# Loads of shifted rows of k from a padded, slice-major copy in DRAM

## The chip, the cores and the metric

The kernel runs on one core of one Trainium2 chip. The metric is the device time of one execution in microseconds (us), as the median of several runs. TensorE is called PE, VectorE DVE, ScalarE ACT, GpSimd POOL and SyncE SP, as in the profile.

## The reference

The reference is one training step of a block: its output and the gradients of nine inputs. With S = 2048 rows, D = 1024 columns and F = 3584:

```python
xn = layernorm(q)                                   # q is also the residual input x
k_shift = sum over t of k_pad[:, t:t+S, :] * shift_k[:, 3 - t]    # k padded by 3 zero rows ahead
kv = k_shift * v
y  = irfft(rfft(kv, 2S) * rfft(ssm_k, 2S))[:S] + kv * ssm_D       # a causal convolution, per column
s  = xn * y
g  = silu(((xn @ w_gate) * (xn @ w_up)) @ w_down)
out = q + s * g
```

`reference` returns `out` and, from `grad_out`, the gradients by q, k, v, shift_k, ssm_k, ssm_D, w_gate, w_up and w_down. All inputs are bf16. k, v and q are [1, 2048, 1024].

What matters here is `k_shift`: row s of it needs the rows s-3, s-2, s-1 and s of k, and the gradient by shift_k needs the same four rows again.

## The kernel before, in words

Rows are laid over the 128 partitions as "(c u r)": half c (2), partition u (128), row r within it (8). So partition u holds 8 consecutive rows of a half, and a tile with shifted rows holds 11: the 8 and the 3 ahead of them.

The program has five stages. The matmuls of each stage are on PE; the convolution's work is threaded through them by a "pump", a generator that is advanced a little at each tick of the main loop.

- Layer norm and the first gate/up units (`layer_norm`, `gu_unit`, lines 399 to 471, called from lines 569 to 587). For each quarter q of the rows, SP loads x, DVE and ACT normalize it, PE transposes it into `XNT`, POOL stores it to `XNd`, and four gate/up units run on that quarter. The x tiles have two buffers, so that a later load waits until an earlier tile has been stored. `build_bcast` (line 124) makes the broadcast weights `Wbc` and `Dbc`; `build_tables` (line 143) makes the transform tables.
- Gate/up matmuls (line 455), with `conv_forward` (line 473) in the pump. The columns are taken in 4 pairs of slices (dp), 8 slices (ds) of 128 columns. `shift(dp)` (line 492) makes acc = k_shift and kv for 256 columns, in two halves c; `load_kv` (line 479) loads k and v for the next half when one is done; `main(ds)` transforms a slice and multiplies, `tail(ds)` ends it. The tile `k` is [128, 11, 256], with one buffer.
- Down projection (line 785), with the pointwise backward and the first part of `conv_backward` in the pump.
- The weight gradients: dh and the gradients of gate and up (lines 891 and 909), then the gradient of w_down (line 952): 56 groups of 16 matmuls into a PSUM bank `psdw`, which ACT copies to a tile `wb` (two buffers) and POOL stores. In the pump runs the rest of `conv_backward` (line 640), and at its end, beside the groups of line 952, `dk_load` (line 727) and `dk_unit` (line 738) for the 8 slices. `dk_load` loads the 11 shifted rows of k (`kh`) and of the gradient of k_shift (`dkh`, from the padded DRAM buffer `DKSHd`) for both halves; each has two buffers. `dk_unit` makes the gradient of k on DVE, in a tile `dka` that has one buffer and is stored half by half, and the gradient of shift_k by 16 matmuls on PE (`psY`, line 755).
- The gradient by q (line 1005).

The loads of k go through `cld_k` (line 64). `cld` is the same as `st` (line 59): a DMA issued by POOL, as all stores are. `ld` (line 56) issues on SP. For half c = 1, `cld_k` issues two DMAs over 128 partitions, for tile rows 0 to 5 and 6 to 10. For c = 0 the first three rows would lie ahead of k, so partition 0 is done apart: a memset of its rows 0 to 2 on DVE, a DMA of one partition for its other 8 rows, and two DMAs over the 127 partitions from 1. Each run in DRAM is one row's w columns: 512 bytes for w = 256, 256 bytes for w = 128.

The framework orders the instructions of each engine itself by a list scheduler with a cost estimate of its own; an engine's queue then runs in that order. So an instruction that stands late in the source (a load of k, a copy) can come early on its engine.

Of the kernel before, what the change touches and what calls it, by code (L numbers as in the profile page):

```python
# [13 lines left out]
BF16 = mybir.dt.bfloat16  # L14
# [5 lines left out]
def build_kernel(  # L20
# [8 lines left out]
    nc = tc.nc  # L29
# [61 lines left out]
    KSHd = dram.tile([4, P, NB, 256], BF16, name="KSHd")  # L91
    KVd = dram.tile([4, P, NB, 256], BF16, name="KVd")
# [31 lines left out]
    def build_bcast(bps):  # L124
# [15 lines left out]
        st(DKSHd[:, S:S + 8, :], zr[:])  # L140
        bsb.release()
# [331 lines left out]
    def conv_forward():  # L473
# [5 lines left out]
        def load_kv(dp, c):  # L479
            d0 = dp * 256  # L480
# [3 lines left out]
            cld_v(v, c, d0, 256)  # L484
            S_["kv", dp, c] = (k, v)
# [6 lines left out]
        def shift(dp):  # L492
            d0 = dp * 256
            kv = cx.tile([P, NB, 256], BF16, name="kv", bufs=1)
            S_["kvt", dp] = kv
            wb = lambda j: Wbc[:, j:j + 1, d0:d0 + 256].to_broadcast([P, 8, 256])
            for c in range(2):
                k, v = S_.pop(("kv", dp, c))
                acc = kst.tile([P, 8, 256], BF16, name="acc")
                tt(acc[:], k[:, 0:8, :], wb(3), MUL)  # L500
                for j in (2, 1, 0):
                    prod = kst.tile([P, 8, 256], BF16, name="prod")
# [3 lines left out]
                tt(kv[:, 8 * c:8 * c + 8, :], acc[:], v[:], MUL)  # L506
                st(KSHd[dp, :, 8 * c:8 * c + 8, :], acc[:])
# [4 lines left out]
            st(KVd[dp], kv[:])  # L512
# [14 lines left out]
        def main(ds):  # L527
            if ds % 2 == 0:
                yield from shift(ds // 2)
            kvs = S_["kvt", ds // 2][:, :, (ds % 2) * P:(ds % 2 + 1) * P]  # L530
# [52 lines left out]
    for q in range(1, 4):  # L583
# [4 lines left out]
        if q == 1:  # L588
            pass
    lns.release()  # L590
    lnp.release()
    build_tables(ps_tr)
# [92 lines left out]
    def dkv_tail(ds, G, ew):  # L685
        e = ds % 2
        for c in range(2):
# [5 lines left out]
            cld(ksh[:], KSHd[ds // 2, :, 8 * c:8 * c + 8, e * P:(e + 1) * P])  # L693
# [422 lines left out]
```

## Time and profile before

| | |
|---|---|
| median of 3 runs | 2884.33 us (2872.3 to 2888.55) |
| the profiled execution | 2892.62 us, its span 2890.8 us |
| PE, DVE, ACT, POOL busy | 2250.8, 1446.9, 859.1, 782.8 us |
| mean granted clock of PE | 0.91 |
| DMA moved | 466.35 MB, 161 GB/s on the mean |
| first and last gate/up matmul (line 455) start | 87.2 and 886.2 us |
| first and last matmul of line 952 start | 1967.7 and 2426.9 us |

The profile is of one execution. A busy share is the time in which an engine had an instruction running. Groups of instructions are named by line, engine, operation and tile, "out<-in"; "<-" behind an idle time names what ended it. In the DMA issues the last number is the median time from issue to landing. The line numbers are those of the kernel before.

### The profile page before, as it was taken

How to read it: one execution, taken by the hardware profiler on the slowest of the kernel's cores; microseconds unless marked ns; L12 is line 12 of the kernel's file. 1: busy time of each engine (PE TensorE's matmuls, PEld its weight loads, DVE VectorE, ACT ScalarE, POOL GpSimd, SP SyncE). 2: the span in 40 equal slices, each digit the busy share in tenths (PEclk: the TensorE clock that was granted, in tenths of full speed). 3: DMA queues.
4: the chain of work that ended last, by engine and by line, in shares of the span. 5: the costliest groups of instructions: out<-in, count | busy, mean ns of one | idle time of the engine just before them, and what ended most of it. 6: DMA issues, size and time to landing. Idle time of an engine off the chain costs nothing.

```text
span 2890.8 us, 35638 instructions
## 1 busy us (share of the span) xinstructions
PE 2250.8 (78%) x14369; PEld 1200.7 (42%) x14634; DVE 1446.9 (50%) x1947; ACT 859.1 (30%) x1204; POOL 782.8 (27%) x990
## 2 busy tenths in 40 slices
PE   0573939859997988599999999999733454899998
PEld 0332515536563444355444554444311122444443
DVE  2532837758775568426775757657222222132222
ACT  1561314324442222343433433543200001221111
POOL 2242222232211433023344343222334432000000
PEclk9886979979998999799999999999866776999999
DMA  3422535354557998645566665555444445652320
GB/s 91 156 91 80 177 114 188 113 168 158 199 182 252 330 327 283 160 143 186 186 198 199 216 198 174 191 208 201 112 71 83 69 70 141 191 181 95 143 97 29
DMA packets 219237, 466.35 MB, mean 161 GB/s; under 512 B 42936, under 2 KB 128000, under 8 KB 206528
## 3 DMA queue, kind: packets, MB, share of 16 engines
q0 software_dynamic: 93440, 266.91, 29.7%
q1 hardware_dynamic: 121472, 195.06, 21.0%
q10 hardware_dynamic: 4160, 2.10, 0.3%
q8 instruction: 114, 1.87, 0.3%
q14 instruction: 51, 0.42, 0.0%
HBM read 273.15 MB, written 189.82 MB: 160 GB/s over the span
## 4 chain that ended last, share of the span: by engine, by line
issue 37%; PE 26%; DMA 13%; DVE 12%; POOL 8%; ACT 3%; POOLq 0%; SPq 0%; DVEq 0%; ACTq 0%
PE psdw L909 9%; DMA kh<-in_A_k_dram 4%; PE psbm L785 4%; DVE W L182 3%; PE psdw L952 3%; PE psdh L891 2%; PE psg L455 2%; POOL kh L60 2%; DMA HFd<-HX 2%; DVE m L182 1%; PE tr L902 1%; POOL out_dram L60 1%; DMA wrow<-DBMd 1%; DVE dgt L182 1%; DMA k<-in_A_k_dram 1%
## 5 line engine op out<-in xcount | busy, mean ns | idle before, releaser
L455 PE MATMUL psg<-XNT,wslab 128*128 128x512 bf16 x1708 | 414.7, 391 | 9.3 <-ACT XNT L442 4.4
L909 PE MATMUL psdw<-dgu,XN 128*128 128x512 bf16 x1740 | 396.7, 379 | 2.7
L952 PE MATMUL psdw<-DBMT,dgu 128*128 128x512 bf16 x874 | 206.0, 393 | 155.7 <-ACT wb L955 154.3
L1005 PEld LDWEIGHTS <-dgut 128*128 128x128 bf16 x1792 | 175.0, 98 | 224.1 <-DMA dgut<-DGUTd 16.7
L455 PEld LDWEIGHTS <-wslab 128*128 128x128 bf16 x1792 | 175.9, 101 | 203.3 <-issue 28.8
L909 PEld LDWEIGHTS <-XN 128*128 128x128 bf16 x1792 | 172.2, 98 | 192.3 <-issue 0.5
L60 POOL DMA_DIRECT2D out_dram<-wb x280 | 151.5, 546 | 295.3 <-ACT wb L913 188.8
L457 ACT CAST gut<-psg 128x512 bf16<-128x512 f32 x224 | 131.1, 586 | 304.6 <-PE psg L455 209.5
L891 PE MATMUL psdh<-DBMT,wdt 128*128 128x512 bf16 x858 | 213.2, 389 | 5.0 <-ACT dht L893 1.4
L182 DVE TENSOR_TENSOR W<-W 128x512 f32<-128x512 f32 (+1 forms) x272 | 213.3, 784 | 7.0
L785 PE MATMUL psbm<-wd,ht 128*128 128x512 bf16 x872 | 200.4, 384 | 9.8 <-DMA ht<-HTd 6.8
L952 PEld LDWEIGHTS <-dgu 128*128 128x128 bf16 x896 | 90.1, 101 | 266.3 <-issue 171.2
L182 DVE TENSOR_TENSOR W<-W,psP 128x512 f32<-128x512 f32 x192 | 122.3, 682 | 121.4 <-PE psP L231 72.5
L1005 PE MATMUL psx<-WGU,dgut 128*128 128x512 bf16 x748 | 168.3, 379 | 1.0
L955 ACT CAST wb<-psdw 128x512 bf16<-128x512 f32 x56 | 32.0, 585 | 395.0 <-DMA out_dram<-wb 284.2
L60 POOL DMA_DIRECT2D kh<-in_A_k_dram x40 | 113.0, 2828 | 128.8 <-issue 122.0
L903 ACT COPY dgu<-tr 128x1024 bf16<-128x1024 bf16 x112 | 113.4, 1012 | 103.0 <-PE tr L902 102.4
L913 ACT CAST wb<-psdw 128x512 bf16<-128x512 f32 x112 | 65.5, 586 | 248.4 <-PE psdw L909 213.3
L182 DVE TENSOR_TENSOR dkp<-dkh,Wbc 128x1024 bf16<-128x1024 bf16 x48 | 33.1, 689 | 208.7 <-DMA dkh<-DKSHd 207.6
L468 PE MATMUL tr<-ident,hT 128*128 128x128 bf16 x448 | 36.9, 224 | 124.4 <-DVE hT L182 123.0
L785 PEld LDWEIGHTS <-ht 128*128 128x128 bf16 x896 | 87.3, 99 | 109.4 <-DMA ht<-HTd 7.0
L1005 PE MATMUL psx<-XN,dgut 128*128 128x512 bf16 x501 | 116.8, 387 | 16.8 <-DMA dgut<-DGUTd 16.3
(217 smaller groups left out, 3339.2 us busy)
## 6 DMA issues: line engine op xcount, KB each, us to landing
ht<-HTd SPq DMA_DIRECT2D x16, 1792.0 KB, 7.8
gul<-GUTd SPq DMA_DIRECT2D x56, 512.0 KB, 4.9
DGUTd<-dgt POOLq DMA_DIRECT2D x56, 512.0 KB, 6.0
dgut<-DGUTd SPq DMA_DIRECT2D x8, 3584.0 KB, 11.9
GUTd<-gut POOLq DMA_DIRECT2D x48, 512.0 KB, 3.3
A<-DYFd POOLq DMA_DIRECT2D x16, 1024.0 KB, 5.5
out_dram<-wb POOLq DMA_DIRECT2D x224, 64.0 KB, 2.2
dgu<-Hd SPq DMA_DIRECT2D x28, 512.0 KB, 5.4
```

What stands on the lines that cost most here:

```text
L60: return nc.gpsimd.dma_start(out=out, in_=in_)
L182: V.tensor_tensor(o, a, b, op)
L455: nc.tensor.matmul(ps[:], w[:, dc, a, fi * P:(fi + 1) * P], XNT[q][:, dc, :], start=(dc == 0), stop=(dc == DC - 1))
L457: nc.scalar.copy(out=gut[:, a, k * 512:(k + 1) * 512], in_=ps[:])
L468: nc.tensor.transpose(ps[:, i, :], hT[:, i * P:(i + 1) * P], ident[:])
L785: nc.tensor.matmul(ps[:], ht[:, fc, i * P:(i + 1) * P], wds[fc // 4][:, fc % 4, :], start=(fc == 0), stop=(fc == NF - 1))
L891: nc.tensor.matmul(ps[:], wdt[:, dc, fi * P:(fi + 1) * P], DBMT[:, dc, s0:s0 + 512], start=(dc == 0), stop=(dc == DC - 1))
L903: nc.scalar.copy(out=dgu[:, :, a, fi * P:(fi + 1) * P], in_=ps[:])
L909: nc.tensor.matmul(ps[:].rearrange("p a f -> p (a f)"), XN[:, b, dc * P:(dc + 1) * P], dgus[b // 8][:, b % 8].rearrange("p a f -> p (a f)" ...
L913: nc.scalar.copy(out=wb[:], in_=ps[:])
L952: nc.tensor.matmul(ps[:], h[:, fi, b, :], DBM[:, b, dh * 512:(dh + 1) * 512], start=(b == 0), stop=(b == NB - 1))
L1005: nc.tensor.matmul(ps[:, dh * 512:(dh + 1) * 512], t[:, a, 4 * j + f, i * P:(i + 1) * P], WGU[j][:, a, f, dh * 512:(dh + 1) * 512], start= ...
```

## The change

A new DRAM buffer `KSLd` of [8, S + 8, 128] holds k by slices of 128 columns, with three zero rows ahead. Eight DMAs from DRAM to DRAM on SP fill it, one for each slice, in runs of 256 bytes at the source; they stand in the source behind the last layer norm and ahead of `build_tables`. One store of zeros by POOL in `build_bcast` fills the rows ahead. `cld_k` is now one DMA over 128 partitions, for either half, with 11 rows of 128 columns in one run of 2816 bytes for each partition; the memset and the one-partition load are gone.

What follows from the layout: the tile `k` is [128, 2, 11, 128] and is loaded by two DMAs, one for each slice of the pair; `shift` works on [128, 2, 8, 128]; `kv` is stored by slices; `KSHd` and `KVd` are by 8 slices of 128 columns and no longer by 4 pairs of 256, and `dkv_tail` and the pointwise stage read them so (`kv_t` by one DMA where there were two).

```diff
-    def cld_k(t, c, d0, w):
-        if c == 0:
-            nc.vector.memset(t[0:1, 0:3, :], 0.0)
-            cld(t[0:1, 3:11, :], kin[0:8, d0:d0 + w].rearrange("(o r) d -> o r d", o=1))
-        p0 = 1 - c
-        for (a, b) in ((0, 6), (6, 11)):
-            off = kin.offset + (1021 * c + 5 * (1 - c) + a) * D + d0
-            cld(t[p0:P, a:b, :], bass.AP(kin.tensor, off, [[8 * D, P - p0], [D, b - a], [1, w]]))
+    def cld_k(t, c, ds):
+        src = KSLd[ds]
+        cld(t, bass.AP(src.tensor, src.offset + 1024 * c * P, [[8 * P, P], [P, 11], [1, P]]))
...
-    KSHd = dram.tile([4, P, NB, 256], BF16, name="KSHd")
-    KVd = dram.tile([4, P, NB, 256], BF16, name="KVd")
+    KSHd = dram.tile([8, P, NB, P], BF16, name="KSHd")
+    KVd = dram.tile([8, P, NB, P], BF16, name="KVd")
+    KSLd = dram.tile([8, S + 8, P], BF16, name="KSLd")
...
         st(DKSHd[:, S:S + 8, :], zr[:])
+        st(KSLd[:, 0:3, :], zr[:, 0:3, :])
...
-            k = kst.tile([P, 11, 256], BF16, name="k")
-            cld_k(k, c, d0, 256)
+            k = kst.tile([P, 2, 11, P], BF16, name="k")
+            for e in range(2):
+                cld_k(k[:, e], c, 2 * dp + e)
...
-                    tt(prod[:], k[:, 3 - j:11 - j, :], wb(j), MUL)
+                    tt(prod[:], k[:, :, 3 - j:11 - j, :], wb(j), MUL)
...
-                st(KSHd[dp, :, 8 * c:8 * c + 8, :], acc[:])
+                st(KSHd[2 * dp:2 * dp + 2, :, 8 * c:8 * c + 8, :].rearrange("e u b d -> u e b d"), acc[:])
...
     lns.release()
     lnp.release()
+    for ds in range(8):
+        ld(KSLd[ds, 3:3 + S, :].rearrange("(p a) d -> p a d", a=16),
+           kin[:, ds * P:(ds + 1) * P].rearrange("(p a) d -> p a d", a=16))
     build_tables(ps_tr)
...
-            cld(ksh[:], KSHd[ds // 2, :, 8 * c:8 * c + 8, e * P:(e + 1) * P])
+            cld(ksh[:], KSHd[ds, :, 8 * c:8 * c + 8, :])
...
-            cld_k(kh[:, c], c, ds * P, P)
+            cld_k(kh[:, c], c, ds)
...
-            kv_t = mi.tile([P, 2, 2, 256], BF16, name="kv_t")
-            for e in range(2):
-                ld(kv_t[:, e], KVd[2 * dh + e, :, 2 * bp:2 * bp + 2, :])
+            kv_t = mi.tile([P, 4, 2, P], BF16, name="kv_t")
+            ld(kv_t[:], KVd[4 * dh:4 * dh + 4, :, 2 * bp:2 * bp + 2, :].rearrange("e u b d -> u e b d"))
```

How the change moves instructions is seen in the engines' order. On SP at the start of the program, before (x are the tiles of the layer norm, in_A_q the input q, wslab the weights of gate and up):

```order
L57 DMA x_135<-in_A_q_dram 128x1024
L57 DMA x_140<-in_A_q_dram 128x1024
L57 DMA x_228<-in_A_q_dram 128x2048
L57 DMA x_467<-in_A_q_dram 128x4096
L57 DMA x_686<-in_A_q_dram 128x4096
L57 DMA x_905<-in_A_q_dram 128x4096
```

and with the change (in_A_k is the input k, KSLd the copy):

```order
L57 DMA x_136<-in_A_q_dram 128x1024
L57 DMA x_141<-in_A_q_dram 128x1024
L57 DMA KSLd<-in_A_k_dram 2048x128 x5
L57 DMA x_229<-in_A_q_dram 128x2048
L57 DMA x_469<-in_A_q_dram 128x4096
L57 DMA KSLd<-in_A_k_dram 2048x128 x3
L57 DMA x_688<-in_A_q_dram 128x4096
L57 DMA x_907<-in_A_q_dram 128x4096
```

The eight copies, which stand behind all layer norms in the source, come on SP ahead of the third and of the fifth x load.

On POOL at the start, before (k is the tile of `load_kv`, XNd the stored layer norm):

```order
L60 DMA XNd<-x_135 128x1024
L60 DMA XNd<-x_140 128x1024
L60 DMA k<-in_A_k_dram 1x8x256
L60 DMA k<-in_A_k_dram 127x6x256
L60 DMA k<-in_A_k_dram 127x5x256
L60 DMA v<-in_A_v_dram 128x4x256 x2
L60 DMA hrow<-in_A_ssm_k_dram 128x2048
L60 DMA XNd<-x_228 128x2048
```

and with the change:

```order
L60 DMA XNd<-x_136 128x1024
L60 DMA XNd<-x_141 128x1024
L60 DMA KSLd<-zr 8x384
L60 DMA v<-in_A_v_dram 128x4x256 x2
L60 DMA hrow<-in_A_ssm_k_dram 128x2048
L60 DMA k<-KSLd 128x1408 x2
L60 DMA XNd<-x_229 128x2048
```

The first k loads are two DMAs over 128 partitions, which wait for the copies of slices 0 and 1 and for the zero rows, and stand behind v and hrow where they stood ahead.

On POOL at one of the slices of `dk_load`, before (wb is the tile of the w_down gradient, dka that of k's):

```order
L60 DMA kh<-in_A_k_dram 1x8x128
L60 DMA kh<-in_A_k_dram 127x6x128
L60 DMA kh<-in_A_k_dram 127x5x128
L60 DMA kh<-in_A_k_dram 128x6x128
L60 DMA kh<-in_A_k_dram 128x5x128
L60 DMA dkh<-DKSHd 128x1408 x2
L60 DMA out_dram<-wb 128x512 x2
L60 DMA out_dram<-dka 1024x1x128 x2
L60 DMA out_dram<-wb 128x512 x2
```

and with the change:

```order
L60 DMA kh<-KSLd 128x1408 x2
L60 DMA dkh<-DKSHd 128x1408 x2
L60 DMA out_dram<-wb 128x512 x2
L60 DMA out_dram<-dka 1024x1x128
L60 DMA out_dram<-wb 128x512 x2
L60 DMA out_dram<-dka 1024x1x128
```

Five loads of k become two for each slice; the stores of `wb` and `dka` alternate behind them as before, with the two halves of `dka` now apart. On PE the order there is the same but for the second slice, whose 16 matmuls of `psY` are no longer split: 64 matmuls of line 952 stand between one slice's `psY` and the next.

More of the change, by code (lines that the diff above doesn't have):

```diff
@@ L479, in load_kv @@
         def load_kv(dp, c):
-            d0 = dp * 256
-            k = kst.tile([P, 11, 256], BF16, name="k")
-            cld_k(k, c, d0, 256)
+            k = kst.tile([P, 2, 11, P], BF16, name="k")
+            for e in range(2):
+                cld_k(k[:, e], c, 2 * dp + e)
             v = kst.tile([P, 8, 256], BF16, name="v")
-            cld_v(v, c, d0, 256)
+            cld_v(v, c, dp * 256, 256)
             S_["kv", dp, c] = (k, v)
@@ L511, in shift @@
                 yield 2.5
-            st(KVd[dp], kv[:])
+            st(KVd[2 * dp:2 * dp + 2].rearrange("e u b d -> u e b d"), kv[:])
         def h_rows(ds):
@@ L529, in main @@
                 yield from shift(ds // 2)
-            kvs = S_["kvt", ds // 2][:, :, (ds % 2) * P:(ds % 2 + 1) * P]
+            kvs = S_["kvt", ds // 2][:, ds % 2]
             yield from h_rows(ds)
@@ L685, in dkv_tail @@
     def dkv_tail(ds, G, ew):
-        e = ds % 2
         for c in range(2):
@@ L831, in build_kernel @@
                     nc.tensor.matmul(psd[:, e, :], dy[:, i, e * P:(e + 1) * P],
-                                     kv_t[:, e // 2, i, (e % 2) * P:(e % 2 + 1) * P],
+                                     kv_t[:, e, i, :],
                                      start=(bp == 0 and i == 0 and e == 0), stop=(bp == 7 and i == 1 and e == 3))
```

15 lines of the change are left out of this document (6 added, 9 removed).

## The prediction

> **What bounds the kernel now.** I read the page first: its busy shares and its slices.
>
> ```profile
> PE 2250.8 (78%) x14369; PEld 1200.7 (42%) x14634; DVE 1446.9 (50%) x1947; ACT 859.1 (30%) x1204; POOL 782.8 (27%) x990
> PE   0573939859997988599999999999733454899998
> ```
>
> TensorE (PE) is busy 78% of a span of 2890.8 us, and the idle time is not spread evenly: it sits at the start, in isolated slices of the first third, and in five slices near three quarters of the span. So I asked the trace for those stretches, beside two without holes.
>
> ```profile
> 36.00:44.00 8.00, 0.00 (x0) 0.00 (x0) 0.00 (x0) 0.00 (x0) 0.00 (x0) 1.00 0.06 18
> 225.00:278.00 53.00, 11.20 (x127) 8.22 (x127) 1.14 (x2) 6.27 (x9) 16.27 (x9) 0.65 0.25 74
> 379.00:432.00 53.00, 7.60 (x39) 3.38 (x37) 7.45 (x10) 3.35 (x5) 12.07 (x10) 0.62 0.36 108
> 560.00:613.00 53.00, 7.28 (x33) 3.12 (x32) 7.35 (x9) 3.35 (x5) 12.05 (x10) 0.61 0.35 107
> 680.00:897.00 217.00, 199.76 (x1756) 126.08 (x1784) 177.82 (x231) 89.30 (x138) 48.55 (x73) 0.98 0.54 182
> 1940.00:2062.00 122.00, 121.35 (x615) 60.84 (x626) 70.61 (x80) 42.93 (x52) 26.46 (x50) 1.00 0.54 191
> 2062.00:2434.00 372.00, 156.60 (x680) 69.42 (x691) 88.03 (x144) 25.41 (x38) 154.34 (x106) 0.72 0.45 78
> ```
>
> The columns after the stretch's length are busy us of PE, weight loads, VectorE (DVE), ScalarE (ACT) and GpSimd (POOL), then the granted clock, the DMA share and GB/s. In the holes all five engines are mostly idle, and the DMA engines move 18 to 108 GB/s; from 36 to 44 us, when nothing runs but a load of k, their share is 0.06, one engine of 16. Beside the holes PE is 92% (199.76 of 217) and 99% (121.35 of 122) busy. Next, who waits for whom. POOL's own rows in one period of the longest hole:
>
> ```profile
> 2237.12 5.66 POOL L60 DMA_DIRECT2D kh<-in_A_k_dram  x1 [0.34 <-issue]
> 2257.03 7.93 POOL L60 DMA_DIRECT2D kh<-in_A_k_dram  x3 [14.25 <-issue]
> 2264.96 1.12 POOL L60 DMA_DIRECT2D dkh<-DKSHd  x2
> ```
>
> and the DMA issues of 2062 to 2434 us (count, KB each, median us to landing):
>
> ```profile
> out_dram<-wb POOLq DMA_DIRECT2D x32, 128.0 KB, 3.4
> out_dram<-dka POOLq DMA_DIRECT2D x16, 256.0 KB, 5.8
> kh<-in_A_k_dram POOLq DMA_DIRECT2D x8, 192.0 KB, 12.5
> kh<-in_A_k_dram POOLq DMA_DIRECT2D x8, 190.5 KB, 19.6
> ```
>
> The loads of 190.5 KB are those of `cld_k` over 127 partitions (127 x 6 runs of 256 bytes). They move 10 GB/s, POOL needs 5.66 us to issue one, and then cannot issue the next for 14.25 us. The `dkh` loads beside them, 128 partitions in runs of 2816 bytes, cost POOL 0.56 us each. POOL issues in order, so the stores of `wb` and the `dkh` loads queue behind, and the waits of 2040 to 2450 us show where that ends:
>
> ```profile
> PE psdw L952 <- ACT wb L955: 154.3, 7, 27.5
> PE psY L755 <- DMA dkh<-DKSHd: 58.9, 2, 32.1
> 2234.30 1.07 ACT L955 CAST wb<-psdw 128x512 bf16<-128x512 f32 x2 [35.38 <-DMA out_dram<-wb]
> ```
>
> PE waits for ACT to empty a PSUM bank, ACT for the store of the last `wb`, that store for POOL.
>
> **The change part by part.** *The dk stretch (2062 to 2434 us).* Every `kh` load becomes a 128-partition load in runs of 2816 bytes, the form of `dkh`: two issues of about 0.56 us a slice where the four large ones took 5.66 + 7.93 = 13.6 us and a 14 us pause. What is late next? PE's own work:
>
> ```profile
> 1988.25 10.74 PE psdw L952 x49
> 2062.00:2434.00 372.00, 121.28 (x497) 52.19 (x508) 0.72 0.45 78
> 2250.17 3.62 PE L755 MATMUL psY<-kh,dkh 128*128 128x512 bf16 x15
> ```
>
> The second row counts line 952 alone: 497 records, which with a few missing is 32 groups of 16 (896 matmuls in all are 56 groups). At 10.74/49 = 0.219 us each they take 512 x 0.219 = 112 us; the eight `psY` groups take 8 x 3.62 = 29 us. PE alone needs 141 us. DVE's whole work there is 88 us (window row), less than that. I add 9 us for the first `dkh` pair and small hand-overs: 150 us, a gain of 372 - 150 = 222 us. Bounds: 141 us at best (gain 231). At worst the slices run in a DVE chain: 88/8 = 11 us of work, then the `dka` store (5.8 us to landing) before the next slice may write `dka`, and one `wb` store's 3.4 us ahead of it in POOL's order, with 3 us for issue and hand-overs: 23 us a slice, 8 x 23 = 184, say 187 us (gain 185).
>
> *The three holes of the forward convolution.* They are the c = 0 loads of column pairs 1 to 3.
>
> ```profile
> PE tr L468 <- DVE hT L182: 115.1, 25, 46.1
> PE psP L231 <- DVE W L182: 45.4, 1, 45.4
> 432.34 1.03 PE L468 MATMUL tr<-ident,hT 128*128 128x128 bf16 x8 [45.69 <-DVE hT L182]
> k<-in_A_k_dram POOLq DMA_DIRECT2D x3, 384.0 KB, 5.5
> k<-in_A_k_dram POOLq DMA_DIRECT2D x3, 381.0 KB, 27.5
> ```
>
> PE loses 45.4, 45.7 and 46.1 us, 137 us together. A 128-partition load of about the same bytes lands in 5.5 us instead of 27.5, and the new ones are two of 352 KB. Without holes, 729 - 137 = 592 us would remain from 168 to 897 us; by the clean stretch's density (92%) the 545.6 us that PE is busy there (window row below) need 593 us, so PE is the next bound and nothing else must move.
>
> ```profile
> 168.00:897.00 729.00, 545.60 (x4663) 341.85 (x4741) 474.17 (x614) 263.14 (x390) 200.48 (x237) 0.88 0.46 152
> ```
>
> I take 130 us, leaving 2 us a hole for the landing of the next load; bounds 110 (DVE, 474 us in 592, now 80% full, in the way) and 137.
>
> *The start.* The first k load and the eight new copies.
>
> ```profile
> 15.99 6.26 POOL L60 DMA_DIRECT2D k<-in_A_k_dram  x2
> 21.23 2.29 DVE L403 TENSOR_REDUCE ssum<-x 128x2 f32<-128x2048 bf16 x1 [4.15 <-DMA x<-in_A_q_dram]
> 69.98 1.23 DVE L182 TENSOR_TENSOR prod<-k,Wbc 128x2048 bf16<-128x2048 bf16 x1 [46.47 <-DMA k<-in_A_k_dram]
> 71.20 4.41 DVE L403 TENSOR_REDUCE ssum<-x 128x4 f32<-128x4096 bf16 x1
> 87.17 3.15 PE L455 MATMUL psg<-XNT,wslab 128*128 128x512 bf16 x7 [1.10 <-ACT XNT L442]
> 96.12 4.41 DVE L403 TENSOR_REDUCE ssum<-x 128x4 f32<-128x4096 bf16 x1
> ```
>
> DVE stands 46.47 us before a `prod` that the scheduler put ahead of the layer norm, and the first gate matmul comes at 87.17, 16 us after the second `ssum` began (71.20). In the new order SP issues five copies ahead of the third x load and three more behind the fourth, so these x loads become the late ones. Their price: a copy is 2048 runs of 256 bytes. No DRAM-to-DRAM transfer is in the trace; its nearest rows are
>
> ```profile
> YFd<-yf POOLq DMA_DIRECT2D x8, 512.0 KB, 5.0
> out_dram<-wb POOLq DMA_DIRECT2D x224, 64.0 KB, 2.2
> q10 hardware_dynamic: 4160, 2.10, 11.3%
> x<-in_A_q_dram SPq DMA_DIRECT2D x1, 1024.0 KB, 7.7
> ```
>
> The store of `yf` has the same size and the same 256-byte runs into DRAM: 5.0 us, of which a small store's 2.2 us is latency, so about 3 us of transfer. ACT's queue in the first 70 us (third row) spent 0.113 x 16 x 70 / 4160 = 0.030 us on each 512-byte packet; 128 packets on each of 16 engines make 3.9 us. I take 3.5 us: five copies 17.5 us, the four weight slabs 4096 x 0.030 / 16 = 7.7 us beside them, all from 1.5 us on, so with the first two x loads they are done at about 28 us; the x loads (7.7 us for the 1 MB one) land at 36, and the first gate matmul comes at 36 + 16 = 52: a gain of 35 us. Bounds: were the copies free, the third x load would land at 21.23 as now and the fourth 7.7 us behind it, at 29, a gain of 42; at twice the price five copies end near 45 and the gain is 18. POOL reaches its k loads at 16 us anyway (first row), when copies 0 and 1, the only ones that they wait for, have landed (1.5 + 7.7 + 2 x 3.5 = 16 us). Queued behind that wait on POOL are the next XNd store and, through its landing, SP's next x load; a microsecond or two there is inside the bounds.
>
> The Trainium skill (DMA: Bandwidth & Descriptors, Specifications) says that transfers below 512 bytes are read-modify-writes, which speaks against copying in 256-byte rows. By that rule a copy would cost about twice, the start would gain 18 and not 35 us, and the time would be 17 us longer; the `yf` row shows no such doubling.
>
> *Edits that I cost at nothing.* DVE's shift now runs over rows of 128:
>
> ```profile
> L182 DVE TENSOR_TENSOR prod<-k,Wbc 128x2048 bf16<-128x2048 bf16 x24 | 29.3, 1222 | 54.6 <-DMA k<-in_A_k_dram 54.4
> L182 DVE TENSOR_TENSOR dkp<-dkh,Wbc 128x1024 bf16<-128x1024 bf16 x48 | 33.1, 689 | 208.7 <-DMA dkh<-DKSHd 207.6
> ```
>
> `dkp` has such rows already: 1222 - 689 = 533 ns for 1024 more elements, so the rate is the same. Were each of the 64 shift operations 10% dearer, it would be 8 us beside PE. The memsets of a row of k go. `KSHd` and `KVd` by slices change run lengths, not bytes; their cover is a PE that is busy while they move, and `kv_t` in one DMA saves 16 issues on SP.
>
> **The rivals.** *A: the dk stretch follows its DVE and store chain* rather than PE: 184 us, as above, 34 us more, 2531 us. For: `dka` has one buffer, and two `dka` products open each slice. Against: the stores of the two halves end at different times.
>
> *B: the copies hold the x loads longer*, at four times my price, 14 us: all eight then end at 1.5 + 112 + 7.7 = 121 us, the second quarter's x load lands behind them at 129 where its `ssum` starts at 96 now, and the start loses 33 us instead of gaining 35: 2565 us. For: no row shows a copy within DRAM. Against: the `yf` row.
>
> *C, the slower end: each copy runs on one engine*, as the 127-partition loads do. Its place is SP's queue ahead of the x loads. At the k load's 27.5/762 = 0.036 us a packet one copy takes 74 us, eight 590 us; the x load behind the last would land at about 598 instead of 96 us, 502 us late, against 352 us gained later: 3034 us. It decides from (352 + 96 - 8)/8 = 55 us a copy. Against: a copy's outer dimension is 2048, and only the loads over 127 partitions show the rate of one engine.
>
> The Trainium skill (same page, "Why a DMA increments its semaphore by 16 and not by 1") has the DMA use the largest number of engines up to 16 that divides the outer dimensions: 1 for 127, 16 for 2048. That agrees with the 10 GB/s above and speaks against C; the exception it names, 127 partitions spread over all 16, isn't what this trace shows.
>
> *D: the loads aren't slow because of 127 partitions*, so the holes stay: about 2885 us. Against: the 192.0 KB loads behind them in the same queue and the `dkh` rows.
>
> **How the numbers follow.** 35 + 130 + 222 = 387 us. The profiled execution took 2892.6 us, 8.3 above the median of the runs (2884.3): 2505.6 for it, 2497 for the median, which I predict. Best ends: 42 + 137 + 231 = 410, from the lowest run (2872.3) 2462. Worst ends: 18 + 110 + 185 = 313, 2571. Chances: forecast 0.74, A 0.15, B 0.07, C 0.02, D 0.02. The range 2455 to 2580 holds the forecast's own, A and B. A measurement of this kernel can tell about 0.5% from no change (the three runs lie within 0.6%). Faster by more than that: 0.96; within it: 0.02; slower: 0.02.
>
> **What would show it.** Right: no `k` or `kh` issue on POOL over 1 us; PE's wait for `wb` in the dk stretch down from 154 us to under 20, and the stretch 141 to 187 us long; no PE wait over 10 us from 168 to 760 us, and the gate stage's end about 165 us earlier; first gate matmul near 52 us. Wrong: copies landing in over 8 us each, `ssum` waiting for x beyond 60 us, or a dk stretch over 200 us with PE waiting for `dkh` or `wb`.

## The result, and the profile after

The changed kernel takes 2483.34 us (median of 4 runs, 2477.21 to 2487.35) beside 2885.07 us for the kernel before (4 runs, 2872.3 to 2888.55): a ratio of 0.8613, 95% interval 0.8579 to 0.8646. The prediction was 2497 us with a range of 2455 to 2580. The profiled execution of the changed kernel has a span of 2485.6 us (before 2890.8) and a mean granted clock of 0.967 (before 0.91).

The page after, PE's and POOL's busy shares and PE's slices of a fortieth of the span each:

```profile
PE 2242.7 (90%) x14634; PEld 1190.7 (48%) x14634; DVE 1445.3 (58%) x1935; ACT 859.8 (35%) x1204; POOL 626.6 (25%) x963
PE   3778999999979894799999999999999978999997
```

PE's and DVE's busy time is what it was (2250.8 and 1446.9 us before): no work went away, waiting did. The five low slices near three quarters of the span are gone, and so are the 3, the 3 and the 5 of the first third. The 4 in the sixteenth slice is a hole that was there before, 181 us later: PE is busy 36.32 us from 932 to 1000 us, where it was 36.29 us from 1113 to 1181 us, in slices that cut it in two. POOL is busy 156 us less, in 990 - 963 = 27 fewer instructions.

Where the 405.2 us of the span lie, by the starts of the first and last matmul of three groups (us):

| | before | after | gained | forecast |
|---|---|---|---|---|
| first gate/up matmul | 87.2 | 48.4 | 38.8 | 35 |
| from there to the last gate/up matmul | 799.0 | 657.2 | 141.8 | 130 |
| from there to the first matmul of w_down's gradient | 1081.5 | 1077.8 | 3.7 | 0 |
| from there to the last of them | 459.2 | 238.4 | 220.8 | 222 |
| sum | | | 405.1 | 387 |

What is left, 0.1 us, lies behind the last of these matmuls. The middle of the program, which the change touches only through layouts, moved by 3.7 us in 1081.5; with the layouts alone (an experiment below) it is 1075.0 us long.

**The gate stage.** The window of this stage in the trace of before (columns as in the prediction: PE, weight loads, DVE, ACT, POOL busy, granted clock, DMA share, GB/s):

```profile
87.00:888.00 801.00, 601.75 (x4936) 367.88 (x5019) 496.24 (x668) 299.63 (x451) 225.76 (x276) 0.88 0.45 150
```

and after; the later rows are the part without the stage's two ends, 87 us ahead of the dk stretch, the dk stretch with a margin, and the dk stretch alone:

```profile
48.00:707.00 659.00, 600.55 (x5020) 363.99 (x5019) 495.03 (x665) 299.63 (x451) 191.16 (x273) 0.96 0.54 182
168.00:680.00 512.00, 484.78 (x4363) 306.07 (x4361) 426.17 (x548) 219.52 (x336) 133.10 (x199) 0.98 0.57 193
1783.00:1870.00 87.00, 87.00 (x451) 43.88 (x449) 58.93 (x68) 31.36 (x38) 16.17 (x30) 1.00 0.52 182
1870.00:2024.00 154.00, 147.65 (x694) 67.63 (x693) 85.86 (x133) 25.38 (x39) 50.33 (x84) 1.00 0.59 183
1877.50:2025.60 148.10, 141.75 (x665) 64.59 (x663) 85.86 (x133) 23.66 (x37) 48.76 (x82) 1.00 0.60 189
```

The stage is 142 us shorter with the same 600 us of PE work; PE's idle time went from 199 to 58 us. From 168 to 680 us PE is 95% busy (484.78 of 512), more than the 92% that the prediction took from the clean stretch of before, with DVE at 83%. PE's waits in this stage before:

```profile
PE tr L468 <- DVE hT L182: 120.8, 27, 46.1
PE psP L231 <- DVE W L182: 45.4, 1, 45.4
```

and after, in the same stage (line 465 is line 468 of before):

```profile
PE tr L465 <- DVE hT L179: 29.8, 31, 4.1
PE tr L438 <- ACT XNT L439: 9.9, 9, 1.1
PE tr L166 <- ACT TI L167: 7.7, 6, 1.6
PE psg L452 <- ACT XNT L439: 4.4, 4, 1.1
```

The three waits of 45 to 46 us are gone, and nothing has taken their place: the longest wait for `hT` is 4.1 us. What stays, 29.8 us in 31 pieces, is what was there beside the holes (120.8 + 45.4 - 137.2 = 29.0).

**The dk stretch.** From the first `kh` issue (1877.5 us) to the end of the last `psY` group (2025.6 us) it is 148.1 us long, where it was 372, and by the last window row PE is busy for 141.75 of them. POOL's rows in one of its periods:

```profile
1901.95 1.18 POOL L60 DMA_DIRECT2D kh<-KSLd  x2
1903.02 1.16 POOL L60 DMA_DIRECT2D dkh<-DKSHd  x2
1904.08 0.63 POOL L60 DMA_DIRECT2D out_dram<-wb  x1
```

the DMA issues of 1870 to 2024 us:

```profile
kh<-KSLd POOLq DMA_DIRECT2D x16, 352.0 KB, 5.2
dkh<-DKSHd POOLq DMA_DIRECT2D x16, 352.0 KB, 5.9
out_dram<-wb POOLq DMA_DIRECT2D x35, 128.0 KB, 4.1
out_dram<-dka POOLq DMA_DIRECT2D x16, 256.0 KB, 3.4
```

and PE's wait for `wb` there, from the view of waits of 1870 to 2030 us, beside DVE's two longest:

```profile
PE psdw L947 <- ACT wb L950: 6.2, 8, 1.2
...
DVE dka L179 <- DMA dkh<-DKSHd: 52.9, 5, 30.1
DVE dka L179 <- DMA out_dram<-dka: 13.7, 4, 6.4
```

`kh` now looks like `dkh`: 0.59 us to issue and 5.2 us to land, and no pause behind it. ACT's `wb`, for which PE waited 154.3 us, costs 6.2 us. DVE waits for loads and for the store of `dka`, but that is idle time beside a PE that is 96% busy, and costs nothing.

**The start.** DVE's and PE's rows of the changed kernel:

```profile
28.97 2.29 DVE L400 TENSOR_REDUCE ssum<-x 128x2 f32<-128x2048 bf16 x1 [11.56 <-DMA x<-in_A_q_dram]
31.18 1.21 DVE L179 TENSOR_TENSOR acc<-k,Wbc 128x2048 bf16<-128x2048 bf16 x1
32.38 4.41 DVE L400 TENSOR_REDUCE ssum<-x 128x4 f32<-128x4096 bf16 x1
...
48.35 7.30 PE L452 MATMUL psg<-XNT,wslab 128*128 128x512 bf16 x21 [1.10 <-ACT XNT L439]
```

and the DMA view of 0 to 60 us (SP's queue with packets, MB and share of 16 engines; then the copies):

```profile
q1 hardware_dynamic: 17232, 7.34, 46.4%
KSLd<-in_A_k_dram SPq DMA_DIRECT2D x8, 512.0 KB, 10.3
```

The wait of 46 us for k is gone, and the third x load is the late one: `ssum` waits 11.56 us for it, and comes at 28.97 instead of 21.23 us. SP issues that load only at 18.82 us, since the five copies ahead of it keep SP from 1.64 to 18.64 us. SP's whole queue, x loads included, took 0.464 x 16 x 60 / 17232 = 0.0258 us a packet, so a copy of 2048 packets on 16 engines costs at most 3.3 us. The first copy is issued at 1.64 us and lands at 11.94, but no 256-byte packet starts before 6.4 us, so the 10.3 us to landing hold time in the queue behind earlier transfers.

### The profile page after: what moved, and what is told of

It reads as the page before. It is cut to its first block, busy times and chain, and to the rows that moved or that the text cites. A ratio compares the mean times of both kernels' runs of the same rounds, so it can differ in the third digit from the quotient of the medians.

```text
span 2485.6 us, 35847 instructions
## 1 busy us (share of the span) xinstructions
PE 2242.7 (90%) x14634; PEld 1190.7 (48%) x14634; DVE 1445.3 (58%) x1935; ACT 859.8 (35%) x1204; POOL 626.6 (25%) x963
## 4 chain that ended last, share of the span: by engine, by line
issue 37%; PE 30%; DVE 14%; DMA 9%; POOL 7%; ACT 3%; POOLq 0%; SPq 0%; DVEq 0%; ACTq 0%
PE psdw L904 12%; PE psbm L781 4%; PE psdw L947 4%; DVE W L179 4%; PE psdh L886 2%; POOL out_dram L60 2%; DMA wrow<-DBMd 2%; PE tr L897 1%; DVE m L179 1%; DVE dgt L179 1%; POOL HTd L60 1%; DMA DGUTd<-dgt 1%; DMA B<-HFd 1%; DVE HX L179 1%; PE psg L452 1%
## 5 line engine op out<-in xcount | busy, mean ns | idle before, releaser
L904 PE MATMUL psdw<-dgu,XN 128*128 128x512 bf16 x1792 | 402.6, 379 | 0.0
L947 PE MATMUL psdw<-DBMT,dgu 128*128 128x512 bf16 x896 | 198.4, 379 | 6.3 <-ACT wb L950 6.2
L908 ACT CAST wb<-psdw 128x512 bf16<-128x512 f32 x112 | 65.7, 587 | 247.0 <-PE psdw L904 210.8
L179 DVE TENSOR_TENSOR dxn<-psx,dxna_t 128x1024 f32<-128x1024 f32 x16 | 19.6, 1224 | 217.9 <-PE psx L1000 217.8
L886 PEld LDWEIGHTS <-wdt 128*128 128x128 bf16 x896 | 85.2, 99 | 88.4 <-issue 7.6
L179 DVE TENSOR_TENSOR dgt<-gul,dht 128x2048 bf16<-128x2048 bf16 x56 | 68.3, 1220 | 98.9 <-ACT dht L888 93.4
L179 DVE TENSOR_TENSOR m<-A,B 128x2048 bf16<-128x2048 bf16 x64 | 75.8, 1221 | 85.4 <-DMA B<-KFd 40.8
```

Source lines behind the costliest of these rows:

```text
L179: V.tensor_tensor(o, a, b, op)
L886: nc.tensor.matmul(ps[:], wdt[:, dc, fi * P:(fi + 1) * P], DBMT[:, dc, s0:s0 + 512], start=(dc == 0), stop=(dc == DC - 1))
L904: nc.tensor.matmul(ps[:].rearrange("p a f -> p (a f)"), XN[:, b, dc * P:(dc + 1) * P], dgus[b // 8][:, b % 8].rearrange("p a f -> p (a f)" ...
L908: nc.scalar.copy(out=wb[:], in_=ps[:])
L947: nc.tensor.matmul(ps[:], h[:, fi, b, :], DBM[:, b, dh * 512:(dh + 1) * 512], start=(b == 0), stop=(b == NB - 1))
```

## The experiments

The theory is the prediction's: a load over 127 partitions runs on one DMA engine. Two rivals stood beside it: the short runs (256 and 512 bytes against 2816) made the loads slow; or the layouts of `KSHd`, `KVd`, `kv` and `kv_t` save the time. The experiments first take the change apart by place, then by cause.

| kernel | median us | ratio to before (95%) |
|---|---|---|
| changed, but `dk_load` as before | 2705.39 | 0.9379 (0.9349 to 0.941) |
| before, the copy used in `dk_load` alone | 2673.13 | 0.9268 (0.9238 to 0.9297) |
| before, with the new layouts alone | 2881.29 | 0.9993 (0.9979 to 1.0007) |
| before, from a padded copy in rows of D | 2491.48 | 0.8634 (0.8617 to 0.8651) |
| changed, half 0 as 127 partitions and one | 2478.08 | 0.8588 (0.857 to 0.8605) |
| before, both halves over 127 partitions | 3323.74 (one run) | |
| before, half 0 in one-row DMAs over 127 | 2482.42 | 0.8612 (0.859 to 0.8634) |
| before, 127 cut into 122 and 5 | 2572.93 | 0.8923 (0.8903 to 0.8943) |
| before, half 0 by 128, 112 and 15, no copy | 2479.07 | 0.8598 (0.8582 to 0.8614) |
| before, half 0 by 128 and three one-row DMAs | 2485.24 | 0.8619 (0.8602 to 0.8636) |
| changed, again, beside the one above | 2485.13 | 0.8622 (0.8606 to 0.8638) |

### The dk stretch as before, in the changed kernel

```diff
         for c in range(2):
-            cld_k(kh[:, c], c, ds)
+            old_k(kh[:, c], c, ds * P, P)
```

`old_k` is the `cld_k` of before.

> The changed kernel, with the loads of k in dk_load alone as before. My accounting: the dk stretch takes back its 221 us, the rest stays: 2690 to 2720 us. If the two parts were not independent (the stretch was slow for another reason, or freed DMA capacity elsewhere pays for it): outside that.

It took 2705.39 us, and PE's wait of before is back:

```profile
PE psdw L957 <- ACT wb L960: 150.2, 7, 26.5
```

Ahead of the dk stretch it is the changed kernel (last gate/up matmul at 707.4 us), and the stretch of w_down's gradient is 458.0 us long again (1786.1 to 2244.1 us, before 459.2). So all but the dk stretch is worth 2884.2 - 2705.4 = 179 us on that chip, by the accounting above 38.8 + 141.8 + 3.7 = 184.

### The copy in the dk stretch alone

```diff
+    for ds in range(8):
+        ld(KSLd[ds, 3:3 + S, :].rearrange("(p a) d -> p a d", a=16),
+           kin[:, ds * P:(ds + 1) * P].rearrange("(p a) d -> p a d", a=16))
...
-            cld_k(kh[:, c], c, ds * P, P)
+            new_k(kh[:, c], c, ds)
```

`new_k` is the `cld_k` of the change; the forward convolution loads as before.

> The kernel before with the copy, whose use is in dk_load alone; forward k loads, KSHd and KVd as before. My accounting: 2885 - 221 = 2664, so 2645 to 2685 us; the copies are hidden behind the wait for the first k load, which stays. If the copies cost time of their own: above 2685.

It took 2673.13 us, 211 less than before. The dk stretch gives its 220 us (w_down's gradient from 1970.6 to 2210.1 us: 239.5), but the start gives 7.6 back, the first gate/up matmul at 94.8 instead of 87.2 us. DVE's rows show why:

```profile
74.29 1.22 DVE L189 TENSOR_TENSOR prod<-k,Wbc 128x2048 bf16<-128x2048 bf16 x1 [56.73 <-DMA k<-in_A_k_dram]
75.43 2.28 DVE L410 TENSOR_REDUCE ssum<-x 128x2 f32<-128x2048 bf16 x1
...
78.83 4.41 DVE L410 TENSOR_REDUCE ssum<-x 128x4 f32<-128x4096 bf16 x1
```

The wait for k is still there, now ahead of both layer norms and ending 4.3 us later (74.29 against 69.98), and the copies do not hide behind it: the fourth x load's `ssum` comes at 78.83 us, where it came at 71.20 before. The two parts together, 179 and 211 + 8 = 219 us, are 398 of some 400 us of the whole.

### The layouts alone

```diff
-    KSHd = dram.tile([4, P, NB, 256], BF16, name="KSHd")
-    KVd = dram.tile([4, P, NB, 256], BF16, name="KVd")
+    KSHd = dram.tile([8, P, NB, P], BF16, name="KSHd")
+    KVd = dram.tile([8, P, NB, P], BF16, name="KVd")
...
-            kv = cx.tile([P, NB, 256], BF16, name="kv", bufs=1)
+            kv = cx.tile([P, 2, NB, P], BF16, name="kv", bufs=1)
...
-            kv_t = mi.tile([P, 2, 2, 256], BF16, name="kv_t")
-            for e in range(2):
-                ld(kv_t[:, e], KVd[2 * dh + e, :, 2 * bp:2 * bp + 2, :])
+            kv_t = mi.tile([P, 4, 2, P], BF16, name="kv_t")
+            ld(kv_t[:], KVd[4 * dh:4 * dh + 4, :, 2 * bp:2 * bp + 2, :].rearrange("e u b d -> u e b d"))
```

All the other edits of layout come with it; k is loaded as before, and there is no copy.

> The changed kernel's layouts (KSHd, KVd, kv, kv_t by slices of 128 columns, the shift on rows of 128) with all loads of k as before and no copy. My accounting: between gate stage and w_down gradients the change gained 3.7 us, so 2875 to 2890 us, not to be told from before. Layout theory: below 2860 us. A dearer shift on DVE: above 2895 us.

2881.29 us over 12 runs, ratio 0.9993 (0.9979 to 1.0007): no difference that could be told. The layouts were rightly costed at nothing.

### 128 partitions, but short runs

```diff
-        if c == 0:
-            nc.vector.memset(t[0:1, 0:3, :], 0.0)
-            cld(t[0:1, 3:11, :], kin[0:8, d0:d0 + w].rearrange("(o r) d -> o r d", o=1))
-        p0 = 1 - c
         for (a, b) in ((0, 6), (6, 11)):
-            off = kin.offset + (1021 * c + 5 * (1 - c) + a) * D + d0
-            cld(t[p0:P, a:b, :], bass.AP(kin.tensor, off, [[8 * D, P - p0], [D, b - a], [1, w]]))
+            cld(t[:, a:b, :], bass.AP(KPd.tensor, KPd.offset + (1024 * c + a) * D + d0, [[8 * D, P], [D, b - a], [1, w]]))
...
+    for i in range(4):
+        ld(KPd[3 + 512 * i:515 + 512 * i, :], kin[512 * i:512 * i + 512, :])
```

`KPd` is k with three zero rows ahead and its rows as they are, so that runs stay 256 and 512 bytes; all else is as before.

> A padded copy of k that stays row-major: the loads go over all 128 partitions, but in the short runs of before (512 and 256 bytes), and all other layouts are those of before. One-engine theory (the cost of before is that a load over 127 partitions runs on one DMA engine and fills its queue, so that POOL can't issue): nearly the whole gain, 2485 to 2520 us; POOL's kh issues near 0.9 us each with no 14 us pause. Run-length theory (the cost is the number of short runs that POOL and the DMA engines must work through): most of the loss stays, over 2700 us. Layout theory (slice-major k, KSHd and KVd bring the gain): 2860 to 2890 us.

It took 2491.48 us, ratio 0.8634. Its `kh` loads, from 1800 to 2040 us:

```profile
kh<-KPd POOLq DMA_DIRECT2D x16, 192.0 KB, 4.3
kh<-KPd POOLq DMA_DIRECT2D x16, 160.0 KB, 4.2
```

192.0 KB in runs of 256 bytes land in 4.3 us, where 190.5 KB over 127 partitions took 19.6. Run length and layouts thus are not the cause. Most of the 6 to 8 us more than the change takes are at the start: the first gate/up matmul is at 54.8 us, not 48.4.

### 127 partitions, but one long run each

```diff
         src = KSLd[ds]
-        cld(t, bass.AP(src.tensor, src.offset + 1024 * c * P, [[8 * P, P], [P, 11], [1, P]]))
+        p0 = 1 - c
+        if c == 0:
+            cld(t[0:1], bass.AP(src.tensor, src.offset, [[8 * P, 1], [P, 11], [1, P]]))
+        cld(t[p0:P], bass.AP(src.tensor, src.offset + (1024 * c + 8 * p0) * P, [[8 * P, P - p0], [P, 11], [1, P]]))
```

> The changed kernel with its long runs, but half 0 of k loaded over 127 partitions and partition 0 apart. One-engine theory: 358 KB in 127 runs go through one engine, 13 to 19 us at 19 to 27 GB/s, against 5 us; with so few runs POOL should not be held for long, so that loads made one slice ahead are partly covered: 2500 to 2580 us, and landing times of 13 us or more for these loads. Run-length theory: as the changed kernel, 2475 to 2495 us.

This one was a surprise: 2478.08 us, ratio 0.8588, not slower than the change. That is the number that the run-length theory gives, which the kernel above speaks against. Its `kh` loads:

```profile
kh<-KSLd POOLq DMA_DIRECT2D x8, 352.0 KB, 5.2
kh<-KSLd POOLq DMA_DIRECT2D x8, 349.2 KB, 4.7
```

The 127-partition load (349.2 KB) lands like its twin of 128: 76 GB/s to landing, against the 18 GB/s at which a lone 127-partition load of before moved from 36 to 44 us. So the theory in its simple form, 127 partitions mean one engine, falls. Two forms of it remained: 127 partitions stay on one engine only where each has several runs; or one engine was at work here too, and long runs are quick on it.

### 127 partitions, short runs, one run each

```diff
         p0 = 1 - c
-        for (a, b) in ((0, 6), (6, 11)):
+        for (a, b) in (((0, 6), (6, 11)) if c else [(r, r + 1) for r in range(11)]):
```

> The kernel before, but half 0 of k loaded by one DMA for each tile row, still over 127 partitions and in the same short runs (127 runs each, 11 DMAs in place of 2). After the long 127-partition loads landed in 4.7 us, 127 partitions alone can't be the cause. Form theory (a load over 127 partitions stays on one engine only when each partition gets several runs): these spread over the engines, land in 2.5 to 4 us, and the time is 2480 to 2530 us. Rival 1, one engine for each such load but another one in turn: landings of 127 x 0.036 + 2 = 5 to 8 us, 2490 to 2560 us. Rival 2, short runs over 127 partitions always go to the same engine: 11 x 4.6 = 50 us for a half of 256 columns as before, 2870 us or more.

This tells the two apart: the runs are short again, the source is k itself, the partitions are 127, and only the number of runs a partition gets from one DMA is now 1. It took 2482.42 us, ratio 0.8612. The `kh` loads:

```profile
kh<-in_A_k_dram POOLq DMA_DIRECT2D x88, 31.8 KB, 2.0
kh<-in_A_k_dram POOLq DMA_DIRECT2D x8, 192.0 KB, 3.2
```

The whole DMA lands in 2.0 us, about the 2.2 us of the 64 KB stores of before. The traces hold every packet that the DMA engines moved, by queue, time and size though not by engine, and its sizes show how the runs were dealt out: among the packets of the 88 loads are 88 of 1796 bytes, that is seven runs of 256 bytes and 4 bytes more. So fifteen engines had eight runs each and one had seven (15 x 8 + 7 = 127). The long loads of the experiment above left the same mark: 16 packets of 2820 bytes, one run of 2816 and 4 bytes, for their 16 loads over 127 partitions. So a DMA over 127 partitions does spread over the engines when each partition has one run. Eleven issues instead of two are not free: the stretch of w_down's gradient is 251.6 us here (1776.6 to 2028.2; this profiled execution took 2491.1 us, the longest of the four), 13 more than with the change; with no copy the start is 5 us earlier (43.1 against 48.4).

### Both halves over 127 partitions

```diff
-            cld(t[0:1, 3:11, :], kin[0:8, d0:d0 + w].rearrange("(o r) d -> o r d", o=1))
-        p0 = 1 - c
+        z = 3 * (1 - c)
+        cld(t[0:1, z:11, :], kin[1021 * c:1021 * c + 11 - z, d0:d0 + w].rearrange("(o r) d -> o r d", o=1))
         for (a, b) in ((0, 6), (6, 11)):
-            off = kin.offset + (1021 * c + 5 * (1 - c) + a) * D + d0
-            cld(t[p0:P, a:b, :], bass.AP(kin.tensor, off, [[8 * D, P - p0], [D, b - a], [1, w]]))
+            off = kin.offset + (1024 * c + 5 + a) * D + d0
+            cld(t[1:P, a:b, :], bass.AP(kin.tensor, off, [[8 * D, P - 1], [D, b - a], [1, w]]))
```

The suspected form is doubled: half 1 needs no partition apart, but is loaded like half 0.

> The kernel before with half 1 of k, too, loaded over 127 partitions and partition 0 apart: the suspected cost is doubled, the bytes and the run lengths stay. One-engine theory: about 40 us more for each of 8 slices in the dk stretch and for each of 3 to 4 column pairs in the forward convolution, 3250 to 3400 us. Run-length and layout theories: 2880 to 2910 us.

One run, 3323.74 us. PE's waits over the whole program, and two POOL rows of the dk stretch:

```profile
PE psdw L952 <- ACT wb L955: 352.2, 7, 60.9
PE tr L468 <- DVE hT L182: 204.9, 28, 46.4
PE psP L231 <- DVE W L182: 130.3, 7, 44.6
...
2497.36 5.64 POOL L60 DMA_DIRECT2D kh<-in_A_k_dram  x1 [10.68 <-issue]
2516.10 6.16 POOL L60 DMA_DIRECT2D kh<-in_A_k_dram  x1 [13.10 <-issue]
```

The holes double with the loads: the gate stage becomes 967.1 us long (168 more, for four more such loads: 42 each), w_down's gradient 729.2 us (270 more, for eight slices: 34 each). Each 127-partition load in the rows above brings POOL's issue of about 6 us and a pause of 11 to 13 us.

One load over 127 x 6 runs has the DMA engines to itself in this trace, from 2267 to 2284.5 us. The DMA view of that stretch:

```profile
DMA packets 784, 0.24 MB, mean 14 GB/s; under 512 B 736, under 2 KB 736, under 8 KB 784
kh<-in_A_k_dram POOLq DMA_DIRECT2D x1, 190.5 KB, 18.2
```

By their sizes, 48 packets carry all the data, 47 of 16 runs (4096 bytes) and one of 10 (2560 bytes). They follow one another over 11 us, 0.234 us for a full one. Beside them run 705 packets of 64 bytes and 15 of 40, which is fifteen times 762 x 4 bytes (the 16 packets left have 4 bytes each). So one engine moves the data, and each of the fifteen others goes through 4 bytes for every one of the 762 runs.

### 122 and 5 partitions

```diff
-        p0 = 1 - c
-        for (a, b) in ((0, 6), (6, 11)):
-            off = kin.offset + (1021 * c + 5 * (1 - c) + a) * D + d0
-            cld(t[p0:P, a:b, :], bass.AP(kin.tensor, off, [[8 * D, P - p0], [D, b - a], [1, w]]))
+        for (p0, n) in (((0, P),) if c else ((1, 122), (123, 5))):
+            for (a, b) in ((0, 6), (6, 11)):
+                off = kin.offset + (1024 * c + 8 * p0 - 3 + a) * D + d0
+                cld(t[p0:p0 + n, a:b, :], bass.AP(kin.tensor, off, [[8 * D, n], [D, b - a], [1, w]]))
```

If the number of engines is the largest up to 16 that divides the partitions, 122 get two and 5 get five; if only 127 (or a prime) were special, 122 would be quick.

> The kernel before, with the 127 partitions of half 0 loaded as 122 and 5; runs and rows for each DMA as before (6 and 5 rows for each partition). It asks how many engines a load with several runs for each partition gets. Divisor theory (the largest number up to 16 that divides the partitions, 122 = 2 x 61, so two engines): 732 runs of 256 bytes over two engines land in 366 x 0.025 + 2 = 11 us where 127 partitions took 19.6, POOL's pause shrinks to some 5 us, and 1342 runs a slice need 17 us, about PE's 17.6: 2500 to 2620 us. Any count that is not a multiple of 16 on one engine: 2870 to 2890 us. Spread over all 16: landing 4 us, 2480 to 2500 us.

It took 2572.93 us (2 runs), ratio 0.8923. The loads and the waits:

```profile
kh<-in_A_k_dram POOLq DMA_DIRECT2D x8, 192.0 KB, 8.8
kh<-in_A_k_dram POOLq DMA_DIRECT2D x8, 183.0 KB, 10.7
...
PE tr L468 <- DVE hT L182: 55.9, 29, 14.0
PE psdw L952 <- ACT wb L955: 26.0, 7, 9.3
```

The 122-partition load of 183.0 KB lands in 10.7 us, where the expectation for two engines was 11. The packets confirm two: the eight such loads of `kh` leave 112 packets of 56 bytes, fourteen for each, and 56 bytes are 4 bytes for each of the last 14 of 366 runs (22 packets of 16 runs, and 14). So fourteen engines go without data, and two share the 732 runs. The longest wait for `hT` is 14.0 us, where one engine gave 46.1 and sixteen give 4.1: a middle number of engines gives a middle time.

### Without a copy at all

```diff
+        def part(p0, n, a, b):
+            off = kin.offset + (8 * p0 + 1024 * c + a - 3) * D + d0
+            cld(t[p0:p0 + n, a:b, :], bass.AP(kin.tensor, off, [[8 * D, n], [D, b - a], [1, w]]))
         if c == 0:
             nc.vector.memset(t[0:1, 0:3, :], 0.0)
-            cld(t[0:1, 3:11, :], kin[0:8, d0:d0 + w].rearrange("(o r) d -> o r d", o=1))
-        p0 = 1 - c
-        for (a, b) in ((0, 6), (6, 11)):
-            off = kin.offset + (1021 * c + 5 * (1 - c) + a) * D + d0
-            cld(t[p0:P, a:b, :], bass.AP(kin.tensor, off, [[8 * D, P - p0], [D, b - a], [1, w]]))
+            part(1, 112, 0, 3)
+            part(113, 15, 0, 3)
+            part(0, P, 3, 7)
+            part(0, P, 7, 11)
+        else:
+            part(0, P, 0, 6)
+            part(0, P, 6, 11)
```

Rows 3 to 10 of the tile exist for all 128 partitions; only rows 0 to 2 need partition 0 apart.

> No copy of k at all: for half 0 the rows that all partitions have (tile rows 3 to 10) are loaded over 128 partitions, and tile rows 0 to 2 over 112 and 15 partitions; short runs as before, all other layouts as before. One-engine theory: the gain of the change without the copies' delay of the third x load (28.97 against 21.23 us), but with more issues on POOL (four for half 0): 2475 to 2510 us. Run-length theory: over 2700 us. Layout theory: 2860 to 2890 us.

2479.07 us, ratio 0.8598. At the start it shows what the copies cost, the third x load's `ssum` at 21.37 us and not at 28.97:

```profile
21.37 2.29 DVE L408 TENSOR_REDUCE ssum<-x 128x2 f32<-128x2048 bf16 x1 [4.18 <-DMA x<-in_A_q_dram]
```

The first gate/up matmul is at 43.7 us, 4.7 earlier than with the change. The second kernel of this kind joins both findings:

```diff
-            part(1, 112, 0, 3)
-            part(113, 15, 0, 3)
-            part(0, P, 3, 7)
-            part(0, P, 7, 11)
+            for r in range(3):
+                part(1, 127, r, r + 1)
+            part(0, P, 3, 11)
```

> A version without the copy, from what the runs have shown: half 0 by three one-row DMAs over 127 partitions and one of eight rows over 128, half 1 as before, all layouts as before. Form theory: no slow load is left and the start isn't delayed by copies: 2470 to 2485 us, first gate matmul near 43 us, at or a few us below the changed kernel. If short runs in the dk stretch cost POOL more than the copies cost at the start: 2485 to 2500 us.

and the changed kernel ran once more on the same chip beside it:

> The changed kernel again, beside e12 on the same chip, to tell the two apart: 2477 to 2490 us.

2485.24 against 2485.13 us: they can't be told apart, and the first lies just past the 2470 to 2485 expected. In the profiled executions it begins 4.0 us earlier (first gate/up matmul at 44.5 against 48.5 us) and gives 2.7 us of that back in the middle (1078.6 us long, with the change 1076.9) and in w_down's gradient (238.4 against 237.4), while the gate stages are alike (659.4 and 659.6). So no version here beats the change by more than a measurement can tell; the one with 112 and 15 partitions and the one with a long run over 127 are 4 to 7 us lower in the median than the change, but weren't run beside it.

## Why the prediction was right, and where it was off

*The mechanism and the sum.* The prediction held: 2497 us forecast, 2483.34 measured. The three terms are 35, 130 and 222 forecast, 38.8, 141.8 and 220.8 measured, and the 3.7 us of the middle were in no term.

*The dk stretch.* Its working held almost to the microsecond: PE's own work 141 us, measured 141.75 in 148.1 us; the 9 us for the first pair and hand-overs are the remaining 6.4. Rival A's chain is in the trace, DVE waiting 13.7 us for stores of `dka`, but it stays beside PE.

*The forward convolution.* Here a term was mis-sized: 141.8 us lie 12 above the 130 taken and 5 above the upper bound of 137. The failing step is "leaving 2 us a hole for the landing of the next load": PE's waits in this stage for `hT` and `W` fell by 166.2 - 29.8 = 136.4 us, so nothing was left in the holes. For the other 5 us the kernel with the layouts alone is the better partner, since its trace has a record of every matmul of the stage where the one of before lacks 84:

```profile
87.00:884.00 797.00, 604.15 (x5020) 366.99 (x5019) 496.32 (x667) 299.79 (x450) 228.49 (x276) 0.88 0.46 151
```

It has the holes, and its stage is 795.1 us long, 137.9 more than with the change. All its waits there come to 191.8 us, with the change to 57.5: 134.3 more. The same 5020 matmuls keep PE busy for 604.15 instead of 600.55 us, 3.6 more, at a granted clock of 0.88 instead of 0.96. So some 4 us are matmuls that ran slower and whose time was counted in no hole; that the lower clock is the reason (0.61 to 0.65 in the holes) fits, and no run varied it by itself. The last 4 us of the 141.8 are the difference between the two profiled executions with holes (799.0 and 795.1 us).

*The start.* Forecast 35, measured 38.8: the first gate/up matmul comes 16 us after the fourth x load's `ssum`, as was said, and that `ssum` begins at 32.38 instead of 36. The price of a copy, 3.5 us, was close: at most 3.3. By the kernel without copies, the five copies ahead of the third x load cost 7.6 us there. Its first gate/up matmul, 43.7 us, is a gain of 43.5, so the bound of 42 for free copies was right within 2 us. The Trainium skill (DMA: Bandwidth & Descriptors, Specifications) has transfers under 512 bytes as read-modify-writes; the copies' packets of 256 bytes took 0.018 us each, beside the 0.030 us of ACT's 512-byte packets before, so this trace shows no doubling.

*What would show it.* The marks that were named came true: `kh` issues of 0.59 us and `k` issues of 0.55, a `wb` wait of 6.2 us, no PE wait over 6.6 us from 120 to 760 us, the gate stage's end 180.6 us earlier (165 forecast), the first gate/up matmul at 48.4 us. One mark was badly put: "copies landing in over 8 us each" came true too (10.3 us) and meant nothing, since the landing time of a queued transfer counts the queue; the copies' rate was the thing to ask for.

*The cause of the slow loads.* The prediction's mechanism is right for the kernel before, but its reason was too wide: the loads are slow not because they cover 127 partitions, but because they cover 127 partitions with several runs each. Rival D, that it isn't the 127 partitions, was half right in that. The shapes side by side, all on POOL:

| partitions x runs | bytes in a run | KB | landed us | engines with data |
|---|---|---|---|---|
| 127 x 6 (before) | 256 | 190.5 | 19.6 | 1 |
| 122 x 6 | 256 | 183.0 | 10.7 | 2 |
| 128 x 6 (copy in rows of D) | 256 | 192.0 | 4.3 | 16 |
| 127 x 1 | 256 | 31.8 | 2.0 | 16 |
| 127 x 1 | 2816 | 349.2 | 4.7 | 16 |
| 128 x 1 (change) | 2816 | 352.0 | 5.2 | 16 |

The engines are worked out from the packet sizes. The loads over 128 partitions leave no 4 bytes for a run, so all sixteen engines carry data there.

The Trainium skill (DMA: Bandwidth & Descriptors, "Why a DMA increments its semaphore by 16 and not by 1") gives a DMA the largest number of engines up to 16 that divides its outer dimension, and names an exception, in which some direct copies issued by GpSimd's queue are dealt over up to 16 engines, 127 partitions over all of them. The first three rows agree with the rule (1, 2 and 16 engines), the fourth and fifth with the exception. The prediction said that the exception isn't what this trace shows; it is there, for partitions of one run. That the number of runs for each partition decides between the two was shown for 127 partitions alone.

The time that POOL takes to issue such a load rises with the runs that each engine has to go through: 0.88 us for 48 runs (128 x 6), 3.02 for 366 (122 x 6), 5.66 for 762 (127 x 6). It isn't a plain rate, since the loads of five rows behind them, with 305 and 635 runs, took 3.26 and 6.18 us. Why POOL can't issue the next one for 11 to 14 us is open: that the 762 entries on every engine fill a queue fits, and no run looked into the queue.

In rival C the 0.036 us "a packet" was the time to landing of a whole load, POOL's issue included, over its runs. The transfer alone is 0.211 us for a packet of 8 runs of 512 bytes, 0.026 us a run, so one engine would have taken some 54 us for a copy and not 74. It changed nothing, since the copies did not stay on one engine.

So neither the long runs nor the copy is needed, and the change does two things of which one would have done: it loads over 128 partitions, which 16 divides (with short runs 2491.48 us), and it gives each partition one run (over 127 partitions 2478.08 us with long runs, 2482.42 us with short ones).

## What to carry to other kernels

When loads of about the same size in one queue differ several times in landing time, compare their shapes: a DMA on POOL over 127 or 122 partitions, with several runs for each, went here through one engine or two, and everything behind it on POOL waited. Ask for such a stretch what the busiest engine has to do in it, since that was the time that remained (141 of 148 us). And before a copy is built, try to cut the load so that all but a few rows cover 128 partitions: here it gave the same time without the copy.

## What the runs showed of the hardware that was not expected

- A DMA over 127 partitions is quick on POOL when each partition gets one run: 349.2 KB in 4.7 us, 31.8 KB in 2.0 us; with 6 runs each, 190.5 KB took 19.6 us.
- In such a slow load one engine moves the data, and each of the other fifteen goes through 4 bytes for every run (705 packets of 64 bytes and 15 of 40 beside 48 packets of data); POOL took 0.88 us to issue a load of 48 runs for each engine and 5.66 us for one of 762.
- Eight copies from DRAM to DRAM in rows of 256 bytes cost at most 3.3 us each for 512 KB, but as they stand ahead of x loads in SP's queue, they moved the third of these by 7.6 us; in the kernel with the copy for the dk stretch alone they were not hidden behind DVE's wait for k either (7.6 us later at the first gate/up matmul).
- In holes of some 50 us the granted clock fell to 0.61 to 0.65; without them the gate stage's is 0.96 instead of 0.88.
